# The second channel product as 49 products of quarters, with right factors made once and read from DRAM for every block

## The chip, the cores and the metric

The kernel runs on one core of one Trainium2 chip. The metric is the device time of one execution in microseconds. Three runs of the kernel before gave a median of 1317.21 us (1316.68 to 1317.98).

## The reference

An attention block in the Performer manner is followed by a Fourier mixing block with a two-layer channel network. All numbers are f32.

```python
q, k, v: (8, 8, 576, 64); omega: (128, 64); w_ch1: (512, 2048); w_ch2: (2048, 512)
h = x @ omega.T - sum(x * x) / 2                     # x = q or k, scaled
phi = exp(h - max(h)) / sqrt(128)
attn = phi(q) @ (phi(k).T @ v) / (phi(q) @ sum(phi(k)) + 1e-6)
x = attn as (8, 576, 512)
u = x + real(fft(fft(x, axis=1), axis=2))
un = (u - mean(u)) / sqrt(var(u) + 1e-6)
out = u + max(un @ w_ch1, 0) @ w_ch2
```

The last line holds most of the arithmetic: 4608 rows go through a product of 512 x 2048 (the first channel product) and one of 2048 x 512 (the second channel product).

## The kernel before

The kernel has an early and a late part. The early part does the attention in 32 pairs of heads (three pairs in flight), the Fourier mixing of each of the eight batches, and the channel network of 512 of the rows in the ordinary way (`plain`, lines 773 to 841: 128-wide matmuls `hp` at line 812, 512-wide `op` at line 835). It also loads both weight matrices, which arrive in 64 bits per number, and makes f32 of them (`narrow`, lines 312 to 331, on ACT, DVE and POOL, through four buffers `slab`). The rows u = x + mixed are written to DRAM (`us`).

The late part takes the other 4096 rows in eight blocks of 512. In each block both channel products are done with Winograd's form of Strassen's method: both factors are cut in half in both directions, and seven products of halves take the place of eight, at the price of sums of halves ahead and behind.

- The first product (`first_of`, lines 955 to 1030) runs over eight chunks `fc` of hidden features. Each gives seven leaves of two 256-wide matmuls (line 966). The sums of the left factor (`w1s`) are made once, those of the rows (`tt`) once per block. Results are saved from PSUM by ACT (line 980), added and cut at zero by DVE (line 953, a custom instruction) or ACT (line 1013), and POOL makes from them the sums that the second product needs (`hs`, line 1030, four instructions of 256 a chunk, one of them in place).
- The second product (`second_of`, lines 1032 to 1111) runs twice per block (i = 0, 1, 256 rows each). Each run has seven products of sixteen 256-wide matmuls (line 1056): 224 instructions in the profile per block, since each f32 matmul stands there as two. The right factors are the weights `w2` in SBUF and three sums of them, `w2s`, made by 16 DVE instructions (line 948) beside the first block. DVE adds every result onto the rows `ur` in SBUF (line 1067), which were loaded from `us`, and SP stores them (line 728).
- The rows of the next block are loaded (`u`, lines 721 and 724), normalized on DVE and POOL (`norm_of`, lines 732 to 759) and turned on PE (line 751) while the second product runs.

What stands on which engine in which order is decided by a planner in the kernel (`Listing`, lines 58 to 137). Every piece of work is a `Step` with an engine, an estimated duration, the events that it waits for and the buffers that it takes and gives; `port=True` marks steps that the planner lets run on only one of DVE and POOL at a time. The planner always places the step that can begin first. The engines then work through their lists strictly in order. Two `set`s of first or second products may be in flight, with eight PSUM banks. DMAs issued from SP stand in SP's list and wait there for what they need.

Of the kernel before, what the change touches and what calls it, by code (L numbers as in the profile page):

```python
# [170 lines left out]
def kernel(  # L171
# [37 lines left out]
    TB = 512  # L209
    NTB = (B * S - NPLAIN * TP) // TB  # L210
# [12 lines left out]
    w2 = const.tile([128, NFC, DM], F32, name="w2")  # L223
# [56 lines left out]
    nc.gpsimd.memset(mhalf[:], -0.5)  # L280
    om2 = fix.tile([128, 2, MF], F32, name="om2")
# [436 lines left out]
    def load_rows(dst, t):  # L718
        b, n = tiles[t]
        if n:  # L720
            nc.sync.dma_start(dst[:], us[b][64 * (n - 1) : 64 * (n + 1), :])
        else:
            for h, u, _, _ in rows_of(t):
                nc.sync.dma_start(dst[h], u)
# [7 lines left out]
    def norm_of(j, t, i, pool, dst):  # L732
# [3 lines left out]
        load_rows(u, t)  # L736
# [106 lines left out]
    def rest(t, yp):  # L843
        yield Step(SP, 0.5, 2.7, take=("ur",), kb=256)
        ur = mlpp.tile([P, DM], F32, name="ur", tag="ur", bufs=1)
        load_rows(ur, t)
        yield Step(DVE, 0.7, after=(("op", t),), give=("bank",))
        nc.vector.tensor_tensor(out=ur[:], in0=ur[:], in1=yp[:], op=ALU.add)  # L848
        yield Step(SP, 0.4, 2.5, give=("ur",), kb=256)
        store_rows(t, ur)  # L850
# [31 lines left out]

    def mixing():
        for b in range(B):
            yield from mix(b)

    def pairs(start):
# [11 lines left out]
        + [block_norms(0, mlpp), plain(), weights()]  # L899
# [14 lines left out]
        bank=8, slab=0, u=2, ht=NFC, hs=HF, ur=4, s=6, set=2,  # L914
    ).items()}
    w1s = late.tile([128, 3, NDC // 2, DFF // 2], F32, name="w1s")
    w2s = late.tile([128, 3, HF, HM], F32, name="w2s")
# [10 lines left out]
    def weight_sums():  # L928
# [10 lines left out]
        for g in range(4):  # L939
            f = slice(HF // 4 * g, HF // 4 * (g + 1))  # L940
            f2 = slice(HF + f.start, HF + f.stop)
            ops = sums_right(
                w2[:, f, 0:HM], w2[:, f, HM:DM], w2[:, f2, 0:HM], w2[:, f2, HM:DM],
                *(w2s[:, i, f, :] for i in range(3)),
            )
            for i, (o, l, r, op) in enumerate(ops):
                yield Step(DVE, 0.7, makes=("w2s", g) if i == 3 else None, port=True)
                nc.vector.tensor_tensor(out=o, in0=l, in1=r, op=op)

    hts, hss = {}, {}  # L950
# [4 lines left out]
    def first_of(j, fc):  # L955
# [4 lines left out]
        lo, hi = (late.tile([128, TB], F32, name="ht2", tag="ht2", bufs=NFC) for _ in range(2))  # L960
        hts[j, fc], hts[j, fc + HF] = lo, hi
# [21 lines left out]
        def added(name, o, ps, with_, give, after=()):  # L983
# [34 lines left out]
            after=tuple((me, c) for c in ("c11", "c12", "c22")),  # L1018
            take=("hs",),
            port=True,  # L1020
        )
        hs = late.tile([128, 3, HT], F32, name="hs", tag="hs", bufs=HF)
        hss[j, fc] = hs
        ops = sums_left(
            lo[:, t1], hi[:, t1], lo[:, t2], hi[:, t2], *(hs[:, i, :] for i in range(3))
# [6 lines left out]
    def second_of(j, i):  # L1032

        t0 = (NPLAIN * TP + TB * j) // 128
        t1, t2 = slice(128 * i, 128 * i + 128), slice(HT + 128 * i, HT + 128 * i + 128)
        me = ("second", j, i)
        urs = []
        for t in (t0 + i, t0 + HT // 128 + i):
            yield Step(SP, 0.5, 2.7, take=("ur",), makes=(me, t))
            ur = late.tile([P, DM], F32, name="ur2", tag="ur2", bufs=4)  # L1040
            load_rows(ur, t)
            urs.append(ur)
        m1, m2 = slice(0, HM), slice(HM, DM)
        yield Step(NONE, take=("set",), after=(("hs", j, 0),))

        def product(ps, left, right, start, after=()):
            for f0 in (0, HF // 2):
                yield Step(
                    PE,
                    1.72,  # L1050
                    after=tuple(("hs", j, f) for f in range(f0, f0 + HF // 2))
                    + tuple(("w2s", g) for g in range(4))
                    + after,
                )
                for fc in range(f0, f0 + HF // 2):
                    nc.tensor.matmul(  # L1056
                        ps[:, 0:HM],
                        lhsT=left(fc),
                        rhs=right(fc),
                        start=start and fc == 0,  # L1060
                        stop=(fc == HF - 1),
                        skip_group_check=True,
                    )

        def added(name, o, ps, give=(), after=()):
            yield Step(DVE, 0.42, 0.1, after=after, makes=(me, name), give=give)
            nc.vector.tensor_tensor(out=o, in0=o, in1=ps[:, 0:HM], op=ALU.add)  # L1067

        def done(*evs):
            yield Step(NONE, makes=evs[0])  # L1070

        yield Step(NONE, take=("bank",))
        x = bank("sx")
        yield from product(
            x, lambda f: hts[j, f][:, t1], lambda f: w2[:, f, m1], True
        )
        yield Step(NONE, makes=(me, "x1"))
        yield Fork(added("p1", urs[0][:, m1], x, after=((me, t0 + i),)))
        yield Step(NONE, take=("bank",))
        z = bank("sz")  # L1080
        yield from product(
            z, lambda f: hss[j, f][:, 0, t1], lambda f: w2s[:, 0, f, :], True
        )
        yield Fork(added("p5", urs[1][:, m2], z, after=((me, t0 + HT // 128 + i),)))
        yield from product(
            x, lambda f: hss[j, f][:, 1, t1], lambda f: w2s[:, 1, f, :], False, ((me, "p1"),)
        )
        yield Fork(added("u2", urs[0][:, m2], x))
        yield from product(
            z, lambda f: hss[j, f][:, 2, t1], lambda f: w2[:, HF + f, m2], False, ((me, "p5"),)  # L1090
        )
        yield Fork(added("c12", urs[0][:, m2], z, ("bank",), ((me, "u2"),)))
        yield from product(
            x, lambda f: hts[j, f][:, t2], lambda f: w2[:, f, m2], False, ((me, "u2"),)
        )
        yield Fork(added("c22", urs[1][:, m2], x))
        yield Step(NONE, take=("bank",))
        y = bank("sy")
        yield from product(
            y, lambda f: hts[j, HF + f][:, t1], lambda f: w2[:, HF + f, m1], True  # L1100
        )
        yield Fork(added("c11", urs[0][:, m1], y, ("bank",)))
        yield from product(
            x, lambda f: hts[j, HF + f][:, t2], lambda f: w2s[:, 2, f, :], False, ((me, "c22"),)
        )
        last = ("ht",) * NFC + ("hs",) * HF if i == HT // 128 - 1 else ()
        yield Step(NONE, give=("set",) + last)
        yield from added("c21", urs[1][:, m1], x, ("bank",))
        yield Step(SP, 0.8, 2.5, give=("ur", "ur"), after=((me, "c11"), (me, "c12")))
        for t, ur in zip((t0 + i, t0 + HT // 128 + i), urs):  # L1110
            store_rows(t, ur)

    def halves():
        for j in range(NTB):
# [3 lines left out]
            for i in range(HT // 128):  # L1118
# [37 lines left out]
```

## Time and profile before

| | |
|---|---|
| time of the profiled execution | 1318.35 us |
| its span, first to last instruction | 1316.6 us |
| PE busy | 1301.3 us, 99% |
| PEld (weight loads, beside PE) busy | 1133.4 us, 86% |
| DVE, ACT, POOL busy | 555.2, 408.7, 296.4 us |
| DMA | 89.66 MB, mean 68 GB/s |
| first 256-wide matmul of the late part | at 522.55 us |
| granted TensorE clock | 1.00 throughout |

The engines are PE (matmuls; PEld its weight loads), DVE, ACT, POOL and SP, which issues most DMAs. An arrow `out<-in` names the tiles that an instruction writes and reads, L12 is line 12 of the kernel. In groups of instructions the numbers are busy time in us, mean ns of one, and the idle time of the engine before them with what ended it. In the chain of waits and in the timeline the columns are start, length in us, engine and what ran. In the view of stretches each engine has its busy time and its number of instructions, and at the end of the row stand the granted clock, the busy share of the 16 DMA engines and GB/s. DMA issues end with the median time from issue to landing. Matmul records end later than the next one begins, so PE's pace is read from start to start. A profile is one execution; its own time stands in the table beside the median of the runs.

### The profile page before, as it was taken

How to read it: one execution, taken by the hardware profiler on the slowest of the kernel's cores; microseconds unless marked ns; L12 is line 12 of the kernel's file. 1: busy time of each engine (PE TensorE's matmuls, PEld its weight loads, DVE VectorE, ACT ScalarE, POOL GpSimd, SP SyncE). 2: the span in 40 equal slices, each digit the busy share in tenths (PEclk: the TensorE clock that was granted, in tenths of full speed). 3: DMA queues.
4: the chain of work that ended last, by engine and by line, in shares of the span. 5: the costliest groups of instructions: out<-in, count | busy, mean ns of one | idle time of the engine just before them, and what ended most of it. 6: DMA issues, size and time to landing. Idle time of an engine off the chain costs nothing.

```text
span 1316.6 us, 20099 instructions
## 1 busy us (share of the span) xinstructions
PE 1301.3 (99%) x7777; PEld 1133.4 (86%) x7777; DVE 555.2 (42%) x1345; ACT 408.7 (31%) x1202; POOL 296.4 (23%) x407
## 2 busy tenths in 40 slices
PE   8999999999999999999999999999999999999998
PEld 7898998888998776888888888888888888888887
DVE  4888687997647420651231231241241241241211
ACT  6766765656655311210210210210210210210210
POOL 2132222241000010440330330330330430430420
PEclk9999999999999999999999999999999999999999
DMA  9545537355232021101101101101101101101101
GB/s 230 173 113 175 166 110 211 113 150 162 64 97 82 26 77 25 48 17 24 57 17 24 57 17 24 56 17 25 56 17 27 54 17 29 52 16 31 35 1 32
DMA packets 82464, 89.66 MB, mean 68 GB/s; under 512 B 42944, under 2 KB 51392, under 8 KB 82368
## 3 DMA queue, kind: packets, MB, share of 16 engines
q1 hardware_dynamic: 77760, 71.59, 20.1%
q0 software_dynamic: 4608, 16.78, 4.1%
q8 instruction: 62, 1.02, 0.3%
q14 instruction: 34, 0.28, 0.1%
HBM read 69.47 MB, written 23.07 MB: 70 GB/s over the span
## 4 chain that ended last, share of the span: by engine, by line
PE 96%; DVE 1%; DMA 1%; ACT 1%; SPq 1%; issue 0%; DVEq 0%; ACTq 0%
PE sx L1056 17%; PE sx L966 16%; PE pp L445 9%; PE sz L1056 8%; PE sz L966 8%; PE kvp L467 5%; PE tps L383 4%; PE hp L812 4%; PE sy L1056 4%; PE sy L966 4%; PE op L835 4%; PE yp L603 4%; PE ndp L508 3%; PE ab L630 2%; PE ndp L516 1%; PE tp L751 1%
## 5 line engine op out<-in xcount | busy, mean ns | idle before, releaser
L411 ACT ACTIVATE e<-pp,nmx 128x128 f32<-128x128 f32 x576 | 157.3, 405 | 43.4 <-DVE nmx L399 43.2
L1030 POOL TENSOR_TENSOR hs<-ht,ht 128x256 f32<-128x256 f32 x64 | 48.2, 753 | 493.9 <-DVE ht L953 493.9
L980 ACT ACTIVATE s<-sx 128x256 f32<-128x256 f32 x128 | 49.0, 384 | 343.8 <-PE sx L966 326.6
L445 PE MATMUL pp<-om,kqT 128*128 128x256 f32 x576 | 137.0, 383 | 1.1 <-ACT kqT L390 1.0
L966 PE MATMUL sx<-unT,w 128*128 128x256 f32 x512 | 131.2, 379 | 0.8 <-DVE ur L848 0.8
L445 PEld LDWEIGHTS pp<-om,kqT 128*128 128x128 f32 x576 | 105.9, 192 | 16.2 <-ACT kqT L390 2.1
L1056 PE MATMUL sx<-w,ht 128*128 128x256 f32 x512 | 114.4, 379 | 0.0
L966 PEld LDWEIGHTS sx<-unT,w 128*128 128x128 f32 x512 | 97.2, 190 | 14.8 <-DVE ur L848 1.6
L399 DVE TENSOR_REDUCE nmx<-pp 128x4 f32<-128x512 f32 (+1 forms) x160 | 95.8, 630 | 28.5 <-PE pp L445 21.6
L1056 PEld LDWEIGHTS sx<-w,ht 128*128 128x128 f32 x512 | 96.7, 190 | 12.9
L953 DVE CUSTOM_DVE_ANT_0 ht<-sz,s 128x256 f32<-128x256 f32 x64 | 27.1, 425 | 184.3 <-PE sz L966 184.3
L331 POOL TENSOR_TENSOR w<-w,raw 128x512 f32<-128x512 f32 x32 | 46.4, 1455 | 176.6 <-DVE raw L329 176.5
L1067 DVE TENSOR_TENSOR ur<-ur,sx 128x256 f32<-128x256 f32 x64 | 27.0, 421 | 139.9 <-PE sx L1056 139.9
L1013 ACT ACTIVATE ht<-sx 128x256 f32<-128x256 f32 x64 | 24.6, 384 | 172.2 <-PE sx L966 172.2
L467 PEld LDWEIGHTS kvp<-vd,e 128*128 128x128 f32 x576 | 72.1, 190 | 3.7 <-issue 0.5
L467 PE MATMUL kvp<-vd,e 128*128 128x130 f32 x576 | 74.4, 275 | 0.0
L966 PE MATMUL sz<-tt,w1s 128*128 128x256 f32 x256 | 65.6, 379 | 1.8 <-DVE w1s L938 1.8
L966 PE MATMUL sx<-tt,w 128*128 128x256 f32 x256 | 65.6, 379 | 1.0 <-DVE ht L953 1.0
L966 PE MATMUL sx<-tt,w1s 128*128 128x256 f32 x256 | 65.5, 379 | 0.0
L966 PE MATMUL sy<-unT,w 128*128 128x256 f32 x256 | 65.5, 379 | 0.0
L966 PE MATMUL sz<-unT,w1s 128*128 128x256 f32 x256 | 65.5, 379 | 0.0
L812 PE MATMUL hp<-unT,w 128*128 128x128 f32 x512 | 61.7, 276 | 0.0
(107 smaller groups left out, 2235.2 us busy)
## 6 DMA issues: line engine op xcount, KB each, us to landing
raw<-in_moe_w_ch_dram POOLq DMA_DIRECT2D x32, 512.0 KB, 6.3
kq<-in_k_dram SPq DMA_DIRECT2D x32, 288.0 KB, 3.0
kq<-in_q_dram SPq DMA_DIRECT2D x32, 288.0 KB, 5.1
vd<-in_v_dram SPq DMA_DIRECT2D x64, 144.0 KB, 4.3
out_dram<-ur SPq DMA_DIRECT2D x72, 128.0 KB, 2.4
u<-us SPq DMA_DIRECT2D x32, 256.0 KB, 4.0
ur<-us SPq DMA_DIRECT2D x32, 256.0 KB, 3.1
uh<-x SPq DMA_DIRECT2D x16, 256.0 KB, 2.0
```

The lines of the kernel that those rows point to most:

```text
L383: nc.tensor.transpose(ps[:, (j - j0) * 128 : (j - j0 + 1) * 128], src(j), ident[:])
L399: nc.vector.tensor_reduce(nmx[:, 0:num], ps[:, 0 : MF * num].rearrange("p (c m) -> p c m", m=MF), axis=AX.X, op=ALU.max, negate=True,)
L411: nc.scalar.activation(out=e[:, c, :], in_=ps[:, MF * c : MF * c + MF], func=AF.Exp, bias=nmx[:, c : c + 1],)
L445: nc.tensor.matmul(ps[:, 256 * j : 256 * j + 256], lhsT=kqT[:, 2 * t + j, :], rhs=om2[:].rearrange("p i m -> p (i m)"),)
L467: nc.tensor.matmul(kvp[:, 0 : 2 * (D + 1)], lhsT=feature(r), rhs=vds[n % NV][:, r, :], start=(r == 0), stop=(r == R - 1),)
L603: nc.tensor.matmul(yp[:, 0:NK], lhsT=fold[:, c, n, :], rhs=tab[:, c, :], start=(c == 0), stop=(c == NC3 - 1),)
L812: nc.tensor.matmul(hp[:, 0:TP], lhsT=w1[:, dc, 128 * fc : 128 * fc + 128], rhs=unTs[key][:, dc, :], start=(dc == 0), stop=(dc == NDC - 1),)
L835: nc.tensor.matmul(yp[:, 0:DM], lhsT=hs[fc][:, 128 * i : 128 * i + 128], rhs=w2[:, fc, :], start=(fc == 0), stop=(fc == NFC - 1),)
L966: nc.tensor.matmul(ps[:, 0:HT], lhsT=left(dc), rhs=right(dc), start=start and dc == 0, stop=(dc == D2 - 1), skip_group_check=True,)
L980: nc.scalar.activation(out=s[:], in_=ps[:, 0:HT], func=AF.Copy)
L1030: nc.gpsimd.tensor_tensor(out=o, in0=l, in1=r, op=op)
L1056: nc.tensor.matmul(ps[:, 0:HM], lhsT=left(fc), rhs=right(fc), start=start and fc == 0, stop=(fc == HF - 1), skip_group_check=True,)
```

## The change

The seven products of halves of the second channel product are each cut in half again in the same way: 49 products of quarters per block, each of four 128-wide matmuls (128 x 128 weights), where 14 products of sixteen 256-wide matmuls were. The two runs of 256 rows become one of 512.

The right factor of each of the 49 is needed in SBUF as 128 x 512 numbers (256 KB). All 49 are made once, in the early part (`w2_parts`): 44 subtractions of 128 x 512 on DVE or POOL, as the planner chooses, in the four `slab` buffers, and SP writes them to DRAM (`w2l`, seven sets of seven, each set waiting until the sums of the set before have landed). The weights `w2` therefore move from the pool that lasts to one of the early part. In the late part SP loads 49 x 256 KB for every block into 15 buffers `wl` (`loads_w2`). `w2s` and its 16 sums go.

The left factors' sums are made from the hidden rows by DVE, four of 128 x 512 for each of the seven products (`add_up`). The results of the leaves are combined in three steps: ACT saves a 128-wide result from PSUM (`save`), DVE adds a later one to it into a tile `part` (`added`), and `part` goes onto the rows `ur2` with 512-wide additions on POOL or DVE (`plus`), 11 per block. The hidden rows stand in one tile `hid`, the sums `hs` in another. Three sets are in flight instead of two.

```diff
+            for o, l, r in ((t1, c12, c11), (t2, c22, t1), (t3, c22, c12), (t4, c21, t2)):
+                yield from op(o, l, r, after=last, makes=("w2t", i) if o is t4 else None)
+            last = (("w2l", i),)
+            yield Step(SP, 2.2, 4.5, after=(("w2t", i),), kb=7 * 256, makes=("w2l", i))
+            for n, t in ((0, c11), (1, c21), (4, c22)):
+                nc.sync.dma_start(w2l[i][n].rearrange("p (f m) -> p f m", f=4), t)
...
-        bank=8, slab=0, u=2, ht=NFC, hs=HF, ur=4, s=6, set=2,
+        bank=8, slab=0, u=2, ht=NFC, ur=3, s=6, set=3, wl=NWL, sums=NSUM, part=4,
...
+    ORDER = (1, 2, 4, 5, 6, 7, 3)
+    PARTS = (1, 2, 5, 6, 3, 7, 4)
+    def loads_w2():
+        for j in range(NTB):
+            for i in ORDER:
+                for n, l in enumerate(PARTS):
+                    yield Step(
+                        SP, 0.45, 2.6, take=("wl",), after=(("w2l", i),), kb=165, makes=("wl", j, i, l)
+                    )
+                    wl = late.tile([128, 4, 128], F32, name="wl", tag="wl", bufs=NWL)
+                    nc.sync.dma_start(wl[:].rearrange("p f m -> p (f m)"), w2l[i][n])
...
+            ops = (
+                (s1, a(1, 0), a(1, 1), ALU.add, 5),
+                (s2, s1, a(0, 0), ALU.subtract, 6),
+                (s3, a(0, 0), a(1, 0), ALU.subtract, 7),
+                (s1, a(0, 1), s2, ALU.subtract, 3),
+            )
+            for o, l, r, op, n in ops:
+                after = ready(0, 1) + ((me, "p5 read"),) * (n == 3)
+                yield Step(DVE, 0.7, after=after, makes=(me, "s", n), port=True)
+                nc.vector.tensor_tensor(out=o, in0=l, in1=r, op=op)
...
+        def save(what, ps):
+            yield Step(ACT, 0.26, 0.1, take=("s",), makes=(me, what))
...
+        def added(what, t, m, ps, with_, give):
+            yield Step(DVE, 0.28, 0.1, after=((me, with_),), makes=(me, what), give=give)
...
+            for f in range(4):
+                nc.tensor.matmul(
+                    ps[:, 0:128],
+                    lhsT=left[:, f],
+                    rhs=wls[j, i, n][:, f],
...
+        yield from leaf(1, x, a(0, 0), True, ready(0), take=one)
+        yield Fork(save("p1", x))
+        yield from leaf(2, y, a(0, 1), True, ready(1), take=one)
+        yield Fork(added("c11", 0, 0, y, "p1", ("bank", "s")))
+        yield from leaf(5, z, s1, True, of_sum(5), take=one, makes=(me, "p5 read"))
+        yield Fork(save("p5", z))
+        yield from leaf(6, x, s2, False, of_sum(6) + ((me, "p1"),))
+        yield Fork(save("u2", x))
+        yield from leaf(3, z, s1, False, of_sum(3) + ((me, "p5"),))
+        yield Fork(added("c12", 0, 1, z, "u2", ("bank", "s")))
+        yield from leaf(7, x, s3, False, of_sum(7) + ((me, "u2"),))
+        yield Fork(added("c22", 1, 1, x, "p5", ("s",)))
+        yield from leaf(
+            4, x, a(1, 1), False, ((me, "c22"),), give=("set", "sums"), makes=(me, "read")
+        )
```

The matmuls of a leaf are at line 1152 of the changed kernel, DVE's sums of the left factors at 1122, its additions at 1135, the wide additions at 1191, ACT's saves at 1130 and the loads at 1087.

On PE, the second product of the first block stood like this before, in the middle of its first run of 256 rows (`sx`, `sy`, `sz` are PSUM banks, `ht` hidden rows, `hs` their sums, `tp` the turning of the next block's rows):

```order
L751 MATMUL tp<-ident,u 128x128 x4
L1056 MATMUL sz<-w2s,hs 128x256 x12
L751 MATMUL tp<-ident,u 128x128 x4
L1056 MATMUL sz<-w2s,hs 128x256 x4
L751 MATMUL tp<-ident,u 128x128 x4
L1056 MATMUL sx<-w2s,hs 128x256 x16
L1056 MATMUL sz<-w_64,hs 128x256 x16
```

Now leaves of up to three products alternate there; these rows are from the fourth, fifth and sixth product of the block (`sums_6459`, `sums_6543` and `sums_6599` belong to them):

```order
L1152 MATMUL sz<-wl,sums_6459 128x128 x4
L1152 MATMUL sx<-wl,hs 128x128 x4
L1152 MATMUL sx<-wl,sums_6459 128x128 x4
L1152 MATMUL sy<-wl,hs 128x128 x4
L1152 MATMUL sz<-wl,sums_6459 128x128 x4
L1152 MATMUL sz<-wl,sums_6543 128x128 x4
L1152 MATMUL sx<-wl,sums_6459 128x128 x4
L1152 MATMUL sx<-wl,sums_6543 128x128 x4
L1152 MATMUL sx<-wl,hid 128x128 x4
L1152 MATMUL sx<-wl,hs 128x128 x4
```

A product's leaves 5, 6, 3, 7 and 4 are rows 1, 3, 5, 7 and 10 here for the fourth product; between two of them on the same bank one leaf or more of another product has been put.

On DVE, the same stage held the additions onto the rows and the next block's norms before (block 1 here):

```order
L741 BN_STATS st<-u 128x6
L742 BN_AGGR mv<-st 128x2
L743 TENSOR_SCALAR rstd<-mv 128x1
L1067 TENSOR_TENSOR ur_6618<-ur_6618,sz 128x256
L747 TENSOR_SCALAR u<-u,mv,rstd 128x512
L1067 TENSOR_TENSOR ur_6622<-ur_6622,sz 128x256
L880 TENSOR_TENSOR tt<-unT_6682,unT_6681 128x512
```

At the start of the stage of the first block there now stand (`sums_6207`, `sums_6276` and `sums_6301` belong to the first three products, `s_...` are saved results):

```order
L1122 TENSOR_TENSOR sums_6301<-hid 128x512
L742 BN_STATS st<-u 128x6
L743 BN_AGGR mv<-st 128x2
L744 TENSOR_SCALAR rstd<-mv 128x1
...
L1135 TENSOR_TENSOR part<-sy,s_6325 128x128
L748 TENSOR_SCALAR u<-u,mv,rstd 128x512
L1135 TENSOR_TENSOR part<-sy,s_6345 128x128
L1122 TENSOR_TENSOR sums_6207<-hid,sums_6207 128x512
```

The sums of the left factors are new in DVE's list, and the last of the first product's four, which leaf 3 needs, stands behind the norms of the next block's rows.

255 lines of the change are left out of this document (154 added, 101 removed).

## The prediction

> **What bounds the kernel now.** I read the page first, then the chain of waits in order of time, then single lines and stretches.
>
> ```profile
> span 1316.6 us, 20099 instructions
> PE 1301.3 (99%) x7777; PEld 1133.4 (86%) x7777; DVE 555.2 (42%) x1345; ACT 408.7 (31%) x1202; POOL 296.4 (23%) x407
> ...
> PE 96%; DVE 1%; DMA 1%; ACT 1%; SPq 1%; issue 0%; DVEq 0%; ACTq 0%
> ```
>
> PE is busy for 99% of the span and holds 96% of the chain that ended last. So time is won only where PE gets less to do, and lost wherever PE starts to wait. The pieces of that chain give PE's real pace, since they go from start to start (start, length, what):
>
> ```profile
> 465.28 14.29 PE hp L812 x128
> ...
> 574.46 5.18 PE sx L1056 x24
> ...
> 590.03 6.91 PE sx L1056 x32
> ...
> 672.91 5.18 PE sx L1056 x24
> ```
>
> 672.91 - 574.46 = 98.45 us is one block of 512 rows. An f32 matmul leaves two records. The second product (L1056, 256 wide) paces at 6.91 / 32 = 0.216 us a record. Line L812 multiplies 128 x 128 by 128 wide in f32, with new weights for each: 14.29 / 128 = 0.1116 us. A leaf of the new product is four such matmuls. Its instructions, by the view of line L1056 (the first and the last of six groups; the four between have 256 each), and one stretch in the steady part:
>
> ```profile
> L1056 PE MATMUL sx<-w,ht x512: 379/379/382, 574.3 to 1297.8; 128*128 128x256 f32 x171
> ...
> L1056 PE MATMUL sx<-w2s,ht x256: 379/379/379, 615.8 to 1311.6; 128*128 128x256 f32 x128
> ...
> 700.00:800.00 100.00, 100.00 (x473) 88.05 (x472) 25.06 (x59) 14.68 (x36) 24.50 (x36) 1.00 0.12 32
> ```
>
> 1792 records, 224 a block. In the stretch PE (first pair of numbers after the length) never idles, DVE works 25 us of 100, POOL 25, the granted clock is 1.00 and DMA is at 0.12. There is nothing to win there but PE work, and much room beside it.
>
> **The change, part by part.**
>
> *PE in the second product.* Removed: 224 x 0.216 = 48.4 us a block. Added: 49 leaves x 4 matmuls x 2 records = 392 x 0.1116 = 43.7 us, a leaf being 0.893 us. The saving is 4.6 us a block, 36.9 us over eight. The first product, the transposes and everything ahead keep their matmuls.
>
> *The hand-overs.* Between leaves, results go through ACT or DVE: a leaf on bank x or z has to wait until the last result there was saved or added. What this takes:
>
> ```profile
> 563.07 1.03 PE L966 MATMUL sz<-tt,w1s 128*128 128x256 f32 x4
> 563.27 0.38 ACT L980 ACTIVATE s<-sx 128x256 f32<-128x256 f32 x1 [0.48 <-PE sx L966]
> ...
> L798 ACT ACTIVATE ht<-hp 128x128 f32<-128x128 f32 x53 | 14.7, 278 | 51.6 <-PE hp L812 51.4
> ...
> L657 DVE TENSOR_TENSOR bmp<-ab,bmp 128x128 f32<-128x128 f32 x32 | 9.1, 284 | 0.0
> ```
>
> ACT starts 0.20 us after PE has gone on to the next group (563.27 against 563.07). A 128-wide PSUM read takes 0.28 us. So a result is out of the bank some 0.5 us after its leaf. In the steady order two leaves (1.79 us) or more stand between leaf 7 of a product (the code's numbers) and leaf 4, which waits for DVE's addition, and between leaf 5 and leaf 3, which waits for a new sum. That holds if DVE is free. What it is given in this stage: 28 sums, 10 of the 11 wide additions, 21 additions of 128 and the next block's norms.
>
> ```profile
> 526.26 0.69 DVE L938 TENSOR_TENSOR w1s<-w1s,w 128x512 f32<-128x512 f32 x1
> 526.87 0.68 DVE L938 TENSOR_TENSOR w<-w 128x512 f32<-128x512 f32 x1
> ...
> 560.55 1.18 POOL L1030 TENSOR_TENSOR hs<-ht,ht 128x256 f32<-128x256 f32 x1
> 561.07 1.21 DVE L948 TENSOR_TENSOR w2s<-w 128x512 f32<-128x512 f32 x1
> ...
> L741 DVE BATCH_NORM_STATS2 st<-u 128x6 f32<-128x512 f32 x36 | 24.8, 688 | 21.4 <-DMA u<-us 21.4
> ...
> L747 DVE TENSOR_SCALAR u<-u,mv,rstd 128x512 f32<-128x512 f32 x36 | 19.6, 544 | 12.8 <-POOL rstd L745 12.3
> ...
> u<-us SPq DMA_DIRECT2D x32, 256.0 KB, 4.0
> ```
>
> A 512-wide sum follows the next one at 0.61 us; beside a POOL sum it takes 1.21. The next block's norms take 4 x (0.69 + 0.54 + 0.61) = 7.4 us and some small instructions, about 9. With 38 x 0.61 and 21 x 0.28 that is 38 us, in a stage of some 46 (leaves and transposes). DVE is no bound, but it works in order, and a turn that finds two sums ahead of it takes 0.20 + 2 x 0.61 + 0.28 = 1.7 us: just the two leaves. The tightest place is the start of the stage: SP issues the loads of u behind two loads that wait for leaf 2 of the first of the seven products, DVE's norm instructions wait for u, and the sum for leaf 3 stands behind them. From the end of leaf 2: some 1.0 us of issue, 4.0 to land, 3 to 3.5 for norms, POOL's power between them and the sum: 8.2 us, needed at about 8.4 (eight leaves, a matmul group and a set of transposes later). I take 0.4 us a block, 3.2 us in all; the ends are nothing (every turn fits) and 3.5 us a block (each of seven products loses 0.5), 28 us. I take the low side because most turns have three leaves or more between them and POOL has few sums left in this stage.
>
> The Trainium skill, page GPSIMD Engine Reference, section 1, says that GpSimd's SBUF interfaces are shared with VectorE, with contention when a DVE instruction has two SBUF inputs. The rows agree (0.61 to 0.69 against 1.21 us). Were all 28 sums hit, DVE would get 28 x 0.6 = 17 us more a block, 55 in a stage of 46, and the sum would come to 1286 + 8 x 9 = 1358 us; POOL's share, 25 us of 100 now and most of it in the first product, speaks against that.
>
> *The loads.* Each leaf needs its 256 KB right factor from DRAM. 15 buffers are filled during the first product; the other 34 start as leaves free them, and four loads of u go between. The last must have landed 48 x 0.893 = 42.9 us after the first leaf starts.
>
> ```profile
> 631.00:632.00 1.00, 1.00 (x7) 0.87 (x6) 0.42 (x1) 0.03 (x1) 0.00 (x0) 1.00 0.95 336
> 632.00:633.00 1.00, 1.00 (x6) 0.90 (x5) 0.42 (x1) 0.00 (x0) 0.73 (x1) 1.00 0.99 356
> ...
> 95.00:100.00 5.00, 5.00 (x69) 4.81 (x68) 4.39 (x10) 2.22 (x7) 4.52 (x4) 1.00 1.18 205
> ...
> GB/s 230 173 113 175 166 110 211 113 150 162 64 97 82 26 77 25 48 17 24 57 17 24 57 17 24 56 17 25 56 17 27 54 17 29 52 16 31 35 1 32
> ```
>
> Bursts of just such loads (128 rows of 2 KB) run at 336 to 356 GB/s: 262,144 B / 346 = 0.76 us each. 38 x 0.76 = 29 us, plus 0.9 for the first leaf and 4.0 to land: 34 us, 9 before they are needed. I cost them at nothing; PE's leaves are the cover. At the 205 GB/s of the last stretch, in which the DMA engines were also full (share 1.18), the cover is gone: first rival. On SP the stores and u loads queue between these loads; with 15 leaves (13.4 us) in hand a wait there of some microseconds reaches nobody.
>
> *The factors made once.* 44 sums of 512, 29 on DVE and 15 on POOL, and 49 x 256 KB of stores go into the attention part after the weights are converted. Removed for it: 16 sums on DVE in the first block, hidden anyway.
>
> ```profile
> 200.00:400.00 200.00, 197.79 (x1630) 172.49 (x1629) 150.88 (x379) 121.50 (x383) 38.31 (x41) 1.00 0.47 131
> ...
> 300.00:450.00 150.00, 149.81 (x1265) 132.52 (x1265) 95.53 (x257) 86.35 (x277) 12.32 (x15) 1.00 0.33 90
> ...
> L383 PE MATMUL tps<-ident,kq 128*128 128x128 f32 x288 | 39.5, 277 | 0.9 <-DMA kq<-in_k_dram 0.9
> ```
>
> From 300 to 450 DVE works 95.5 of 150 us. 29 sums of 0.69 to 1.21 us make it 116 to 131. In 200 to 400, with DVE as full (151 of 200) and conversions on POOL, PE lost 2.2 us. So 2 us; the ends are -0.2 (the idle time there is all that could be got back) and 29 x 0.69 = 20 us, if each sum delayed PE by its length. The stores stand on SP ahead of later loads of k, q and v and wait there for the sums; behind them PE's transposes would wait. PE lost 0.9 us to those loads in all, and there are two buffers, so nothing is taken; uncovered, a set of seven stores at 205 GB/s would hold the queue for 9 us.
>
> *Start and end of the late part.*
>
> ```profile
> 522.55 1.99 PE L966 MATMUL sx<-unT,w 128*128 128x256 f32 x8 [0.78 <-DVE ur L848]
> 526.33 1.97 PE L966 MATMUL sz<-tt,w1s 128*128 128x256 f32 x8 [1.78 <-DVE w1s L938]
> ...
> 536.21 1.99 PE L966 MATMUL sx<-tt,w 128*128 128x256 f32 x8 [1.01 <-DVE ht L953]
> ...
> 1311.99 0.42 DVE L1067 TENSOR_TENSOR ur<-ur,sx 128x256 f32<-128x256 f32 x1 [3.03 <-PE sx L1056]
> ```
>
> With three sets in flight instead of two the last of the three gaps at the start should close: -1.0 us (0 to -3.6, all three). At the end one addition of 0.42 becomes an ACT copy of 0.28, a hand-over and a DVE sum of 0.69: +0.7. And there leaves 7 and 4 of the last product stand next to each other with nothing between: +0.6. Together +1.3.
>
> *Sum.* The profiled execution took 1318.35 us (span 1316.6 and 1.75 around it). 1318.35 - 36.9 + 3.2 + 2.0 - 1.0 + 1.3 = 1286.9 us. The median of the runs shown, 1317.21, lies 1.1 below that execution, so I forecast 1286 us.
>
> **The rivals.**
>
> 1. *The loads set the pace: slower.* If the stream holds 205 GB/s, a load takes 1.28 us and 38 take 48.6; with 4.9 for the first leaf and the landing the last leaf could start at 53.5 instead of 42.9. 10.6 us a block against the 4.6 saved is +6.0, 48 us in all: 1317.2 + 48 + 2.3 (start, end, attention part) = 1368 us. It decides from 0.9 + 4.0 + 38 t = 42.9 + 4.6, t = 1.12 us, 234 GB/s. For it: the page's fullest slice moved 230 GB/s. Against: that slice held rows of 256 B, and the 336 to 356 above are of this very shape. The Trainium skill, page DMA: Bandwidth & Descriptors, section Anatomy of one DMA, gives about 2.0 us of fixed cost for each DMA plus its bytes at 436 GB/s. By that, an estimate, 2.6 us for 256 KB, and with loads one behind the other 34 of them would take 88 us, slower by far; the 0.76 us in the bursts show that here they overlap. Chance 0.06.
>
> 2. *DVE takes PE's place in part.* Turns lose 0.3 us in each of seven products beside POOL's work, and the sums of the first three products, which stand behind the next block's norms, come 1 us late: 3 us a block. 8 x (4.6 - 3.0) = 12.8 less 2.3 of the other terms: 1307 us. For it: DVE goes from 25% to over 80% in this stage. Against: two to four leaves between most turns. Chance 0.12, 0.02 that it eats just the gain (about 1317), and 0.01 for more.
>
> 3. *The attention part pays.* DVE's 29 sums push the softmax maxima back by most of their 20 us: 1286 + 18 = 1304 us. Against: the stretch 200 to 400. Chance 0.05.
>
> That the matmuls are not cut as said can be left out: the order on PE shows 49 groups of four 128-wide matmuls a block.
>
> **How the numbers follow.** Forecast 1286 us, chance 0.74; its own range takes 1277 (no stall, nothing lost in the attention part, all of the start won) to about 1298. A measurement here tells 0.2% (2.6 us) from no change. Faster: 0.74 + 0.12 + 0.05 = 0.91, of which 0.01 goes to same, for a gain that just fails: 0.90; same 0.02 + 0.01 = 0.03; slower 0.06 + 0.01 = 0.07. The range from 1277 to 1308 takes in the forecast and rivals 2 and 3 and leaves out rival 1 and the tails.
>
> **What would show it.** Right: a block of 93.8 to 94.5 us from second product to second product; the new leaf at 0.893 us; PE idle in the second product under 1 us a block, with DVE as its releaser; DMA near 300 GB/s in bursts but not full; the span up to the first 256-wide matmul of the first product longer by 0 to 4 us. Wrong: PE waiting for DMA wl (rival 1); PE waiting some 3 us a block for DVE sums or part (rival 2); that first matmul later than 530 us (rival 3); or a leaf paced above 0.91 us, which would mean that line L812 is no measure for it.

## The result and the profile after

The changed kernel took 1286.95 us (median, 1285.80 to 1289.02) beside 1317.45 us (1316.68 to 1317.98) for the kernel before on the same chip: ratio 0.9771, 95% interval 0.9754 to 0.9788, 30.5 us less. Timed again later it was 1287.25 beside 1318.65, 0.9760 (0.9746 to 0.9773). The profiled execution took 1289.02 us, the longest of the four. Its page:

```profile
span 1287.3 us, 24674 instructions
PE 1267.3 (98%) x9121; PEld 1144.5 (89%) x9121; DVE 765.8 (59%) x1723; ACT 470.5 (37%) x1424; POOL 332.6 (26%) x427
...
PE 94%; DVE 3%; DMA 1%; ACT 1%; SPq 1%; issue 0%; DVEq 0%; ACTq 0%
```

DVE went from 555 to 766 us of work and ACT from 409 to 471, and still PE holds 94% of the chain that ended last. The pieces of that chain (start, length, what):

```profile
511.91 13.75 PE op L836 x32
...
589.47 3.57 PE sx L1152 x32
...
675.32 2.68 PE sx L1152 x24
...
863.48 2.68 PE sx L1152 x24
...
957.35 2.68 PE sx L1152 x24
```

A leaf record (L1152) paces at 3.57 / 32 = 0.1116 us, and a block takes 957.35 - 863.48 = 93.87 us, where it took 98.45: 8 x 4.58 = 36.6 us won. The two blocks from 675.32 to 863.48 took 188.16, 0.4 more than twice that. The last piece of plain work on PE (op) starts at 511.91 instead of 508.04: the early part is 3.9 us longer. The late part as one stretch, from its first 256-wide matmul to its last matmul, first before, then after (length, then busy time of PE, PEld, DVE, ACT and POOL, the clock, the DMA share and GB/s):

```profile
522.55:1311.97 789.42, 786.62 (x3696) 691.64 (x3696) 208.86 (x475) 114.92 (x284) 197.20 (x284) 1.00 0.11 31
```

```profile
526.42:1280.81 754.39, 750.59 (x5040) 702.86 (x5040) 398.10 (x822) 176.45 (x507) 215.00 (x289) 1.00 0.52 168
```

PE idles 3.80 us there instead of 2.80. DVE's work nearly doubled, by 189 us, the DMA traffic went from 31 to 168 GB/s, and hardly any of it reaches PE. PE waits before a leaf twice in all (us in total, times, longest), once for a sum and once in the last pair:

```profile
PE sx L1152 <- DVE part L1135: 0.4, 1, 0.4
PE sz L1152 <- DVE sums L1122: 0.2, 1, 0.2
```

No load of a right factor is among these. The waits of SP's queue show the reverse: a load waits for the leaf that frees its buffer, 208 times for bank sx alone (365.2 us in total). And the page has the median way of a load from issue to landing:

```profile
wl<-w2l SPq DMA_DIRECT2D x392, 256.0 KB, 3.6
```

The three idle places of PE at the start of the late part, in the timeline (start, length, engine and line, what, and in brackets the idle time ahead):

```profile
526.42 1.99 PE L1009 MATMUL sx<-unT,w 128*128 128x256 f32 x8 [0.78 <-DVE ur L849]
...
530.27 1.97 PE L1009 MATMUL sz<-tt,w1s 128*128 128x256 f32 x8 [1.86 <-DVE w1s L994]
...
540.51 1.13 PE L1009 MATMUL sx<-unT,w 128*128 128x256 f32 x4 [1.36 <-ACT s L1023]
```

And the end:

```profile
1279.40 4.98 SPq L729 DMA_DIRECT2D out_dram<-ur  x8
1279.65 1.16 PE L1152 MATMUL sx<-wl,hs 128*128 128x128 f32 x8 [0.38 <-DVE part L1135]
...
1281.20 0.69 DVE L1191 TENSOR_TENSOR ur<-ur,part 128x512 f32<-128x512 f32 x1 [1.61 <-ACT part L1184]
```

The last matmul ends at 1280.81, 6.5 us ahead of the end of the span. Before it was 1311.97, 4.6 us ahead. The stores that wait for the last sum, first before, then after:

```profile
1312.44 1.11 SPq L728 DMA_DIRECT2D out_dram<-ur  x2
```

```profile
1281.93 2.45 SPq L729 DMA_DIRECT2D out_dram<-ur  x4
```

Set side by side in the profiled executions (us):

| term | predicted | measured |
| --- | --- | --- |
| PE work of the second product | -36.9 | -36.6 |
| hand-overs between leaves, the last two among them | +3.8 | +0.6 (idle 3.80 - 2.80, less 0.4 at the start) |
| start of the late part | -1.0 | +0.4 (1.86 + 1.36 against 1.78 + 1.01) |
| factors made once, in the attention part | +2.0 | +3.9; +1.5 when profiled again; +1.7 timed alone |
| from the last matmul to the end | +0.7 | +1.9 |
| sum | -31.4 | -29.8; the spans differ by 29.3, and 0.5 is not traced |

### The profile page after: what moved, and what is told of

The parts are those of the page before. It is cut to its first block, busy times and chain, and to the rows that moved or that the text cites. A ratio compares the mean times of both kernels' runs of the same rounds, so it can differ in the third digit from the quotient of the medians.

```text
span 1287.3 us, 24674 instructions
## 1 busy us (share of the span) xinstructions
PE 1267.3 (98%) x9121; PEld 1144.5 (89%) x9121; DVE 765.8 (59%) x1723; ACT 470.5 (37%) x1424; POOL 332.6 (26%) x427
## 4 chain that ended last, share of the span: by engine, by line
PE 94%; DVE 3%; DMA 1%; ACT 1%; SPq 1%; issue 0%; DVEq 0%; ACTq 0%
PE sx L1009 17%; PE sx L1152 15%; PE pp L446 9%; PE sz L1009 8%; PE sz L1152 8%; PE kvp L468 5%; PE tps L384 4%; PE hp L813 4%; PE sy L1009 4%; PE op L836 4%; PE yp L604 4%; PE sy L1152 4%; PE ndp L509 2%; PE ab L631 2%; PE ndp L517 1%; PE tp L752 1%
## 5 line engine op out<-in xcount | busy, mean ns | idle before, releaser
L1071 POOL TENSOR_TENSOR hs<-hid 128x256 f32<-128x256 f32 x64 | 46.4, 725 | 404.4 <-DVE hid L997 404.4
L997 DVE CUSTOM_DVE_ANT_0 hid<-sz,s 128x256 f32<-128x256 f32 x64 | 27.2, 425 | 161.1 <-PE sz L1009 153.5
L1152 PE MATMUL sx<-wl,sums 128*128 128x128 f32 x896 | 113.4, 275 | 0.0
L1152 PE MATMUL sz<-wl,sums 128*128 128x128 f32 x896 | 113.2, 275 | 0.2 <-DVE sums L1122 0.2
L1152 PEld LDWEIGHTS sz<-wl,sums 128*128 128x128 f32 x896 | 107.1, 192 | 0.8 <-ACT s L1130 0.4
L1152 PEld LDWEIGHTS sx<-wl,sums 128*128 128x128 f32 x896 | 107.0, 192 | 0.3
L1130 ACT ACTIVATE s<-sx 128x128 f32<-128x128 f32 x112 | 31.1, 278 | 116.5 <-PE sx L1152 83.2
L1152 PE MATMUL sx<-wl,hid 128*128 128x128 f32 x512 | 67.4, 275 | 0.0
L1056 ACT ACTIVATE hid<-sx 128x256 f32<-128x256 f32 x64 | 24.6, 384 | 116.1 <-PE sx L1009 94.2
L1152 PEld LDWEIGHTS sx<-wl,hid 128*128 128x128 f32 x512 | 62.7, 192 | 0.5
```

The source lines that it names most:

```text
L1152: nc.tensor.matmul(ps[:, 0:128], lhsT=left[:, f], rhs=wls[j, i, n][:, f], start=start and f == 0, stop=(f == 3), skip_group_check=True,)
```

## The experiments

My theory was: the gain is PE work alone, all that the change adds lies beside it. The rivals were loads that set the pace, DVE in PE's place, and a dear attention part. Twelve runs, each timed beside the kernel before; us given without a name are medians.

**The making of the factors alone** (e1_parts_alone): the kernel before with `w2_parts` added to it.

```diff
-        + [block_norms(0, mlpp), plain(), weights()]
+        + [w2_parts(), block_norms(0, mlpp), plain(), weights()]
```

> The kernel before, with only the new making of the 49 right factors added in the attention part (44 sums, 49 stores of 256 KB); nothing reads them. Theory: the attention part pays a few us for them, 2.0 by the prediction, 3.9 by the two profiled executions (the first 256-wide matmul of the first product at 526.42 us against 522.55): 1319 to 1321.5 us. Rival: those 3.9 us are scatter between executions or belong to another order of the later work, and the sums and stores cost nothing: 1317 to 1318 us, with that matmul at 522 to 523. Third rival of the prediction: 1330 us and more.

1319.9 beside 1318.24, ratio 1.0014 (1.0005 to 1.0024): 0.7 to 3.2 us more, and the medians differ by 1.7. Third rival out. Its last piece of op on the chain:

```profile
513.35 13.75 PE op L835 x32
```

Profiled, it is 5.3 us late, so one profiled execution is no measure for a term of this size.

**The changed kernel again** (e0_changed_again), no edit.

> The changed kernel once more, as the measure for the two runs beside it and for the spread of its parts from one execution to the next. All theories: 0.975 to 0.979 of the kernel before, 1286 to 1290 us. Theory on the attention part (its making of factors costs 1 to 3 us; 3.9 in the first profiled execution were partly scatter): the last piece of op on the chain starts between 509 and 513 us here. Rival (3.9 us are its price each time): at 512 or later.

1287.25, ratio 0.9760 (0.9746 to 0.9773). In the chain:

```profile
509.52 13.75 PE op L836 x32
```

1.5 us late this time, with the same instructions as in the execution with 3.9. The prediction's 2.0 stands.

**Eight buffers for the loads** (e2_ring8).

```diff
-    NWL, NSUM = 15, 3
+    NWL, NSUM = 8, 3
```

> The changed kernel with 8 buffers for the loaded right factors instead of 15. Theory (loads of 0.76 us each stream behind the leaves): 41 + 4 loads from the first leaf on, 0.9 + 4.0 + 45 x 0.76 = 39.1 us, less than the 42.9 at which the last is needed, so no change: 1285 to 1289 us. Rival: the stream holds only 295 GB/s, what the fullest slices of the page after moved, 0.89 us a load: 4.9 + 45 x 0.89 = 44.9, 2.0 us late in each block, 1303 us. At 205 GB/s (1.28 us): 19.6 us late, 1440 us.

1314.3, ratio 0.9966 (0.9953 to 0.9979): 27 us slower than with 15. My theory of the cover fell, and no rival had this price. Two places of a block in the chain, then two of PE's waits (us in total, times, longest):

```profile
680.53 3.18 DMA wl<-w2l
...
703.58 3.92 DMA wl<-w2l
```

```profile
PE tp L752 <- DVE u L748: 6.8, 5, 2.1
PE sx L1152 <- DMA wl<-w2l: 3.4, 7, 1.0
```

The chain passes through single loads on their way (3.2 and 3.9 us), not through a stream that is too slow. With the other two banks PE waits 4.2 us for loads, and 6.8 us where the transposes of the next block's rows wait for their norms, whose loads of u stand in the same queue of SP. All of PE's waits behind the start of the late part come to 14.6 us; the other half of the 27 is not traced to a wait. By the program's order the loads go product by product, while PE mixes the leaves of three products: a leaf may be far ahead in use of its place among the loads. With eight buffers the planner also mixes less.

**Eight buffers, loads in the order of use** (e9_ring8_by_use). `USE` is the order of the 49 leaves on PE in the changed kernel, written out.

```diff
+    NWL, NSUM = 8, 3
...
-            for i in ORDER:
-                for n, l in enumerate(PARTS):
+            for i, l in USE:
```

> The run with 8 buffers took 27 us more. Its loads go product by product, but PE mixes the leaves of three products: the 9th leaf of a block there is the 15th that is loaded, so that only two leaves, 1.8 us, are left for a landing of 3.4. Here the loads stand in the order in which PE uses them, with 8 buffers and the leaves of PE in the order of the changed kernel. Theory: 7 leaves, 6.2 us, lie between release and use, more than the 0.5 for the issue and 3.6 to land: 1284 to 1289 us. Rival (eight buffers are too few whatever the order, since stores and loads of u hold the queue or the stream is too slow): 1300 to 1315 us.

1287.8, ratio 0.9770 (0.9756 to 0.9783): as the changed kernel, with half the buffers. So neither the stream nor the depth was short, the order of the loads was. (The expectation counted two leaves for the case before; load 15 needs seven buffers freed, so only the eighth leaf, 0.9 us, lay between.) The chain of this run:

```profile
579.02 2.68 PE sx L1158 x24
...
587.96 6.38 DMA wl<-w2l
...
673.42 2.68 PE sx L1158 x24
```

One load among those of u took 6.4 us and came just in time; the block took 94.4 us.

**Four buffers** (e3_ring4), the loads product by product.

```diff
-    NWL, NSUM = 15, 3
+    NWL, NSUM = 4, 3
```

> The changed kernel with 4 buffers for the loaded right factors: the cover of the loads is taken away. Theory: now the way from issue to landing decides. A buffer comes free after its leaf, is asked for some 0.3 us later and filled 3.6 us after that (the page's median), and only three leaves, 2.7 us, lie between: four leaves take 0.9 + 0.3 + 3.6 = 4.8 us instead of 3.57, 12 x 1.2 = 15 us a block, 1405 us; PE waits for DMA wl. If the 3.6 us are mostly queueing behind other loads and a lone one lands in 2.5, four leaves take 3.7 us: 1.5 us a block, 1299 us. Rival (bytes alone count, not the way): 49 loads x 0.76 = 37 us fit into 44, 1285 to 1290 us.

1385.35, ratio 1.0504 (1.0484 to 1.0524): 98 us more than the changed kernel, 12.3 a block, 1.0 us for four leaves where the theory had 1.2. The longest and the shortest of the loads on its chain:

```profile
932.39 4.68 DMA wl<-w2l
...
1027.31 2.57 DMA wl<-w2l
```

With the cover gone the way from issue to landing counts, not the bytes. The Trainium skill, page DMA: Bandwidth & Descriptors, section Anatomy of one DMA, gives about 2.0 us and the bytes at 436 GB/s, an estimate of 2.6 us for 256 KB (it states this for DMAs that GpSimd issues); the 2.57 agrees, and the others are longer.

**Loads left out** (e7_loads_left_out).

```diff
-        for j in range(NTB):
-            for i in ORDER:
-                for n, l in enumerate(PARTS):
+        for n, l in enumerate(PARTS):
```

> The changed kernel without its loads: the seven right factors of one product are loaded once, and every product uses them (what is left out: the other 385 loads, so that all products but those of the first kind take a wrong right factor). Theory: the loads cost PE nothing but a late u in one or two blocks (2.2 us): 1283 to 1287 us. Rival: they cost more by contention on SP's queue, in memory or on the way of u, ur and the stores, spread where no wait shows it: under 1280 us.

1293.32, ratio 0.9811 (0.9798 to 0.9825): 6 us more, which neither theory had. The run is no clean measure of the loads: the planner, free of them, put PE's leaves in another order. Its chain:

```profile
677.53 2.68 PE sx L1148 x24
...
689.99 0.98 DVE u L748
...
691.31 0.61 DVE sums L1118
...
772.48 2.68 PE sx L1148 x24
```

A block takes 94.95 us in that order, 1.1 more, and its chain leaves PE for DVE's norms of the next block and the sums among them. That the loads cost nothing is borne out by this run only so far as leaving them out won nothing. The better witness is the block of the changed kernel with its loads: 98.45 less the 4.6 of PE work saved is 93.8 us, and it took 93.87.

**Two products in flight** (e4_two_sets).

```diff
-        bank=8, slab=0, u=2, ht=NFC, ur=3, s=6, set=3, wl=NWL, sums=NSUM, part=4,
+        bank=8, slab=0, u=2, ht=NFC, ur=3, s=6, set=2, wl=NWL, sums=NSUM, part=4,
```

> The changed kernel planned with two products in flight instead of three. Theory: the hand-overs between leaves are covered by leaves of the other products; with one other product a turn has one or two leaves (0.9 to 1.8 us) against the 0.5 us of a plain hand-over and the 1.7 us of one that finds two sums ahead on DVE: two of seven products lose 0.8 us, 1.6 us a block, 1300 us (1288 to 1310), with PE waiting in the second product for DVE part, DVE sums or ACT s. Rival: they are hidden whatever the order, and the third set did nothing: 1285 to 1288 us, PE idle in the second product 1.6 us in all as with three.

1297.86, ratio 0.9840 (0.9825 to 0.9855): 11 us more than with three, the theory's size. Its chain, and the largest of PE's waits:

```profile
780.45 2.68 PE sx L1152 x24
...
875.79 2.68 PE sx L1152 x24
```

```profile
PE tp L752 <- DVE u L748: 6.8, 7, 1.0
```

A block is 95.34 us, 1.5 more. The largest part is not between leaves, as I had it: PE's transposes wait for DVE's norms of the next block, six times in the late part, 6.1 us together (the seventh, of 0.7 us, lies in the early part).

**One sum more, and three more, for each product** (e5_one_sum_more, and e6_three_sums_more with `range(3 if n == 7 else 0)`). The extra sums overwrite part of that product's result, so its values are not the reference's; the work and its order are.

```diff
                 nc.vector.tensor_tensor(out=o, in0=l, in1=r, op=op)
+                for _ in range(1 if n == 7 else 0):
+                    nc.vector.tensor_tensor(
+                        out=part[:].rearrange("p t m -> p (t m)"),
+                        in0=w1[:, 0, 0:512], in1=w1[:, 0, 512:1024], op=ALU.add,
+                    )
```

> The changed kernel with one more sum of 512 on DVE in each of the 56 products (of two parts of the first weights, into a buffer that is written over later), the order otherwise the same: DVE gets 7 x 0.61 = 4.3 us a block more, 42 of the 46 us of its stage. Theory (DVE has room and works in order): a turn that now finds three sums ahead takes 0.20 + 3 x 0.61 + 0.28 = 2.3 us, more than the two leaves of the tightest turns; one or two such turns a block, 0.5 us each: 1287 to 1295 us. Rival 2 of the prediction (DVE's work takes PE's place): each sum in full, 8 x 4.3 = 34 us, 1321 us. Rival (every turn has room): 1285 to 1288.

> As the run with one sum more, with three in each product, one behind the other: 12.8 us a block more, 38 + 12.8 = 51 us of work for DVE in a stage of 46. Theory: DVE is now the bound there and can catch up a little in the first product: 5 us a block at least, and a turn behind three extra sums takes 2.3 us and more in each of seven products (0.5 to 1 each), 5 to 10 us a block together: 1327 to 1367 us, PE waiting for DVE sums and part. Rival 2 (DVE already full with the change): 8 x 12.8 = 102 us, 1389 us. Rival (DVE works ahead in the first product): under 1300.

1299.47, ratio 0.9855 (0.9842 to 0.9869): 12 us, 1.5 a block, for 4.3 us of sums; above my 1287 to 1295, far from the 34 of rival 2. With three 1373.28, ratio 1.0422 (1.0407 to 1.0438): 86 us, 10.8 a block, for 12.8 us of sums; above my 10. Part of the second price is PE's own. A wait of it in the timeline, one of five alike, each in another block:

```profile
596.75 3.75 PE L1157 MATMUL sz<-wl,sums 128*128 128x128 f32 x16 [4.84 <-DVE sums L1122]
```

The stretches around it (the clock is the number behind the five engines):

```profile
591.91:596.75 4.84, 0.01 (x1) 0.04 (x1) 4.77 (x7) 0.28 (x1) 1.70 (x1) 0.86 0.45 163
596.00:600.00 4.00, 3.25 (x15) 3.29 (x16) 2.43 (x6) 0.00 (x0) 0.55 (x1) 0.50 0.05 13
600.00:604.00 4.00, 4.00 (x28) 4.00 (x27) 2.94 (x8) 0.28 (x1) 0.72 (x1) 0.72 0.60 172
```

After 4.84 us without work the granted clock is 0.50, and 0.72 over the next four us: half for 2.2 of these, until 602.2. From 596.75 on that is 5.5 us at half clock, 2.7 us of matmul time lost on top of the wait. The first row puts the fall inside the wait: 0.86 over 4.84 us is half clock for the last 1.4, so the clock fell some 3.5 us after the last matmul and stayed at half for 6.8 us in all. The next two blocks have two waits of 3.1 to 3.2 us each instead, the last block none of this length. If five blocks lose 2.7 us, the price without it is (86 - 13.5) / 8 = 9.1 us a block, if seven do, 8.4; either is inside the theory's 5 to 10. So the room that DVE has in its stage is 4.3 - 1.5 = 2.8 us a block by the one run, 12.8 less 9.1 or 8.4, some 4, by the other. This is an estimate: it takes every us beyond the room for one of PE's, and each sum at 0.61 us.

**Mends at the edges** (e10_edges): loads in the order of use, with 15 buffers; two of a block's four loads of u asked for ahead of its slabs; the last sum and its stores cut into two row tiles.

```diff
+        if j:
+            for t in (t0, t0 + 1):
+                yield from load_u(t, pool, ("u", t))
...
+        if last_one:
+            yield Fork(half(0, after=((me, "c11"), (me, "c12")), makes=("half", 0)))
```

> The changed kernel with three small mends at the places where its profile shows PE idle or the end late: loads of the right factors in the order of use, two of the four loads of u of the next block asked for ahead of its slabs, and the last sum and its stores cut into two row tiles, so that two stores instead of four stand behind the last sum. Theory: from the last matmul to the end of the span 4.6 to 5.2 us instead of 6.5, the wait of PE for DVE u (2.2 us in one block) gone: 2 to 4 us less than the changed kernel beside it, 1283 to 1286. Rival (these waits are not on the path that sets the end, or come back elsewhere): within 1 us of it.

1325.16, ratio 1.0047 (1.0034 to 1.0061): 38 us slower than the changed kernel. Its chain:

```profile
710.11 2.68 PE sx L1170 x24
...
808.94 2.68 PE sx L1170 x24
```

The place in one block's timeline:

```profile
979.52 3.48 DVE L1140 TENSOR_TENSOR sums<-hid 128x512 f32<-128x512 f32 x3
...
981.00 0.52 SPq L722 DMA_DIRECT2D u<-us  x1
...
985.67 0.69 DVE L751 BATCH_NORM_STATS2 st<-u 128x6 f32<-128x512 f32 x1 [0.45 <-DMA u<-us]
...
987.28 0.66 PE L761 MATMUL tp<-ident,u 128*128 128x128 f32 x4 [1.93 <-DVE u L757]
...
993.52 2.02 PE L1170 MATMUL sz<-wl,sums 128*128 128x128 f32 x16 [2.26 <-issue]
```

A block takes 98.83 us, 4.9 more. The first two norms come earlier, but the third and fourth u still need the buffers of the first two; their norms now stand between DVE's sums and wait there for a load that is issued at 981.00 and used at 985.67, and PE's transposes and the sums behind those norms are late. The next run keeps the order of the loads and the cut sum and loses nothing, so the price is that of the u loads. What they were to remove was not there: the changed kernel's one wait of PE for a norm (DVE u, 2.2 us) ends at 236.66, in the early part, and its second profile has none. The cut at the end brought nothing: from PE's last matmul to the end 6.5 us as in the changed kernel, since SP gave out the eight stores in one row, 4.97 us.

**Last stores on two engines** (e12_last_stores): loads in the order of use, the u loads as in the changed kernel, the last sum cut, three of the eight last stores issued by ACT.

```diff
+            yield Fork(store_half(1, (0,), SP, nc.sync, (("second", j, 3), "done")))
+            yield from store_half(0, (0, 1), ACT, nc.scalar, ("half", 0))
+            yield from store_half(1, (1,), ACT, nc.scalar, (("second", j, 3), "done"))
```

> The changed kernel with the loads in the order of use and another end; nothing of the u loads is moved. The last sum is cut into two row tiles, and of the eight last stores five stay on SP and three go out from ACT behind its last copy. In the run with the three mends the cut alone left 6.5 us from the last matmul to the end, since SP gave out the eight stores one behind the other, 4.97 us from the first on. Theory (the queue of eight stores sets the end, 0.62 us each): SP is through with five 3.1 us after the first, ACT with its three some 1.9 us after its copy, and the end comes 1 to 2.5 us nearer to the last matmul, 4.0 to 5.5 us; 1284.5 to 1287 us. Rival (the landing of the last store sets it, or stores from two engines wait for each other): 6 us and more, 1286 to 1289 us. The order by use alone: no difference.

1285.71, ratio 0.9760 (0.9747 to 0.9773), the same as the changed kernel by that measure. Its end:

```profile
1279.01 2.42 SPq L729 DMA_DIRECT2D out_dram<-ur  x4
...
1279.27 1.16 PE L1158 MATMUL sx<-wl,hs 128*128 128x128 f32 x8 [0.38 <-DVE part L1141]
...
1280.61 1.86 ACTq L1257 DMA_DIRECT2D out_dram<-ur  x3
```

From the last matmul (1280.43) to the end of the span (1286.1) 5.7 us: between theory and rival. The last store is given out 2.0 us behind the last matmul (1282.47) instead of 3.6 (1284.38), but then it is 3.6 us to the end instead of 2.9. One queue was part of the end, not all of it.

**All rows in blocks** (e11_no_plain_rows), nine of them.

```diff
-    NPLAIN = 4
+    NPLAIN = 0
```

> The changed kernel with all 4608 rows in blocks of 512 (nine), none in the plain tiles of 128. Theory (PE work alone counts): 512 plain rows take 4 x (14.29 + 13.75) = 112.2 us of PE, a block 93.9: 18 us less, 1269 us. Rival (the plain tiles fill places in the attention part in which PE would wait for DVE and ACT): some 50 us of their matmuls lie there, 261 records of 0.112 and 48 of 0.43; if half of those places stay empty, 1287 - 18 + 25 = 1294 us; if all, 1319 us. DVE, busy for 83 to 94% between 50 and 300 us, speaks for the rival.

1315.07, ratio 0.9972 (0.9960 to 0.9984): 28 us more than the changed kernel, near the rival in which all those places stay empty. The stretch from 300 to 450 us, here and then in the changed kernel:

```profile
300.00:450.00 150.00, 132.64 (x1085) 116.29 (x1085) 107.65 (x280) 79.03 (x253) 25.12 (x26) 0.94 0.51 161
```

```profile
300.00:450.00 150.00, 148.91 (x1252) 130.03 (x1251) 104.82 (x261) 85.67 (x277) 28.31 (x26) 1.00 0.54 165
```

Without the plain rows PE idles 17 us of 150 there instead of 1, and the mean granted clock is 0.94. In the chain the first block's second product starts so much earlier:

```profile
509.84 2.68 PE sx L1152 x24
```

581.45 - 509.84 = 71.6 us (69.5 by the execution with 579.06) for 112 us of plain work taken out, and a ninth block adds 93.9. PE waits for many things in the attention part, the longest time for the norms of the first block (DVE u, 10.8 us); DVE as a whole is not full (108 of 150). The plain tiles are dearer in PE work, and right where they fill gaps.

## Why the prediction was right, step by step

*PE in the second product.* -36.9 predicted, -36.6 measured. Line L812, a matmul of the same shape elsewhere in the kernel, gave the leaf's pace to four digits (0.1116), and the chain's start-to-start pieces gave the block. This one term carries the result.

*The hand-overs.* +3.8 with the last pair, +0.6 measured. The term was sized too high, by the fear of the place where the sums stand behind the next block's norms; in the changed kernel's chain it lost 0.4 us in one block of eight. But the place is as tight as said: other orders cost 1.1 us a block (no loads), 1.5 (two sets) or 4.9 (u earlier). And "DVE is no bound" held with a small margin: DVE works 38.4 of the 48.9 us from the second leaf of a block to its last (860.67 to 909.61), 4.3 us more cost 1.5, 12.8 more cost 10.8. How far POOL slows the sums shows in two groups of the changed kernel's late part, those that read hid (three of the four such products come first in a block) and those that read hs:

```profile
L1122 DVE TENSOR_TENSOR sums<-hid 128x512 f32<-128x512 f32 x64 | 49.8, 806 | 0.3
...
L1122 DVE TENSOR_TENSOR sums<-hs 128x512 f32<-128x512 f32 x48 | 32.9, 685 | 0.0
```

0.81 and 0.69 us on average, where a sum beside POOL took 1.21. The rule of the Trainium skill (GPSIMD Engine Reference, section 1, shared SBUF interfaces) shows in the groups that read hid alone, and far from the 17 us a block that it would cost if all sums were hit. The two other groups that read hid (32 sums each) took 0.84 and 0.73; above 0.69 the three groups come to some 14 us in all, 1.7 a block.

*The loads.* Costed at nothing, and that is what they took. The step behind it failed all the same: "with 15 leaves (13.4 us) in hand" is not so. By the program's order the sixth leaf of a block is the 15th that is loaded, the eighth the 16th and the tenth the 17th, which can go out when the second leaf is done. The trace has this as the shortest lead (the tenth leaf is the second half of the PE row):

```profile
861.75 0.32 SPq L1087 DMA_DIRECT2D wl<-w2l  x1
```

```profile
867.78 1.95 PE L1152 MATMUL sz<-wl,sums 128*128 128x128 f32 x16
```

From 861.75 to 868.67 it is 6.9 us, in every block, half of the 13.4. Against a landing of 2.4 to 5.7 us (median 3.6) that was enough; the run with eight buffers showed where it ends, and the run with loads in the order of use showed why. The first rival's ground, a stream at 205 GB/s, did not appear: with eight buffers in the right order a block still takes 94.4 us.

*The attention part.* +2.0; 1.7 timed alone, between 0.7 and 3.2. DVE's 29 sums took 0.68 us each. From 300 to 450 us, where 28 of them lie, its work came to 104.8 us and not to 116 to 131, since other work of DVE moved behind them (23.6 us instead of 9.9 from 450 to 520).

*Start and end.* The start was wrong in sign, by 1.4 us. A third set did not close the third gap: it moved it to ACT, where a copy waits for a buffer that DVE frees behind the first weights' sums. At the end the copy and the sum came as priced (+0.6), but from the last sum to the end it is 5.4 us instead of 4.2 (1281.89 to 1287.3, 1312.41 to 1316.6): four stores wait for the last sum where two did, and these 1.2 us I had not counted.

*The sum.* That the forecast lies within 1 us of the median is in part luck: 3.2 us too much for the hand-overs stood against 1.4 too little at the start, 1.2 at the end and up to 1.9 for the factors.

## What to carry to other kernels

Price a new matmul shape by a line of the same shape in the same trace, start to start, and the sum is done before any doubt about the rest. Count a ring of buffers in the order of use and not in the order of loading: eight in the right order did what eight in the wrong order missed by 27 us. Where an engine that works in order is four fifths full, its sequence can matter more than its load, and moving a load earlier can cost more than the wait that it was to remove.

## What was not expected of the hardware

PE pays twice for a long wait. In the run with three sums more the granted clock fell to 0.50 some 3.5 us into a wait of 4.84 us and was back at 1.00 only 5.5 us after the wait. In the changed kernel PE's waits in the late part are 1.9 us at most, and the clock stays at 1.00. The Trainium skill, page TensorE: Matmul & The Clock Gate, Part 1, says that an idle window of some 3.4 us halves the clock and a busy one brings it back, and that the window runs freely; the trace agrees: half, 3.5 us to the fall, and 6.8 us at half, two such windows.

SP needs about 0.62 us to give out one store (eight in 4.98 us), so that the four stores that wait for the last sum take 2.45 us, where that sum takes 0.69.
